# A recurrent-memory attention with a gated MLP: the output projection's last set in two column parts, K's first set inside the first Q group, the second selection in another PSUM bank

## The chip, the cores and the metric

The kernel runs on one core of a Trainium2 chip. The metric is the device time of one execution in microseconds (us); less is better. The core's engines are TensorE (PE in the profile; PEld for its weight loads), VectorE (DVE), ScalarE (ACT), GpSimd (POOL) and SyncE (SP), which issues most DMAs. They run at the same time and wait for each other by semaphores: counters that an engine raises when an instruction ends, and that another engine's instruction waits to reach a value. SBUF is the working memory. PSUM is the small memory that matmuls write; it has 8 banks here, each 512 fp32 columns wide on 128 partitions.

## The reference, cut to what matters

A sequence of 2048 tokens is cut into 64 segments of 32. Each segment is attended together with 8 memory rows, and the first 8 rows of a segment's output projection are the next segment's memory. So each segment starts only when the one before has ended. The MLP branch and the gate do not depend on that recurrence.

```python
def _A_ref(x, mem0, Wq, Wk, Wv, Wo, seg_len):
    ...
    mem = mem0
    outs = []
    for s in range(n_seg):
        xs = x[:, s * seg_len:(s + 1) * seg_len, :].copy()
        h = jnp.concatenate([mem, xs], axis=1)
        q = jnp.einsum('btd,dhe->bhte', h, Wq)
        k = jnp.einsum('btd,dhe->bhte', h, Wk)
        v = jnp.einsum('btd,dhe->bhte', h, Wv)
        scores = jnp.einsum('bhqe,bhke->bhqk', q, k) * scale
        scores = jnp.where(mask[None, None], scores, -1000000000.0)
        p = _softmax(scores, axis=-1)
        o = jnp.einsum('bhqk,bhke->bhqe', p, v)
        o = jnp.einsum('bhte,hed->btd', o, Wo)
        mem = o[:, :M, :].copy()
        outs.append(o[:, M:, :])
    return jnp.concatenate(outs, axis=1)
...
x = A_x
g = _sigmoid((x * gate_w).sum(-1, keepdims=True))
a = _A_ref(x, A_mem0, A_Wq, A_Wk, A_Wv, A_Wo, A_seg_len)
b = _B_ref(x, B_w1, B_b1, B_w2, B_b2)
return g * a + (1 - g) * b
```

There are 32 heads of 128 channels, the model width is 512, and M is 8.

## The kernel before, in words

The kernel has two stages. The first (to about 90 us) runs the MLP of some of the token tiles and loads the weights; the second is the loop over the 64 segments (line 756), which fills the rest. The order of work on every engine is the order in which the program was written: nothing is rescheduled. The framework adds the semaphore waits.

A tile T is 128 tokens, so four segments (si = 0 to 3). A segment's 32 working rows are the 8 memory rows and its first 24 tokens; the last 8 tokens of the four segments of a tile ("left" tokens) are worked on together, ahead of time, as filler work. The tile `hT` (three copies: `hc` is this segment's, `hn` the next one's) holds the 32 rows transposed, in four blocks of 128 model channels, kc = 0 to 3. Its columns 24 to 31 are the memory, written by the boundary described below.

The unit of TensorE work is a **set**: four matmuls with 32 columns of weights each, on the four column groups of the array, that run beside each other and write the four 32-partition quarters of one PSUM bank. A segment does, in this order:

1. Q and K (lines 777 to 786). Four groups, Q of heads 0 to 15 in bank U[0], K of these in U[1], Q of heads 16 to 31 in U[2], K of these in U[3]; each group is four sets, one for each kc (`qk_unit`, line 125), of 512 columns. When a group is complete ScalarE casts the bank (`qk_cast`, line 133) and VectorE transposes it into QT or KT (`qk_tr`, line 137). After the first group VectorE puts a mask into U[0] (`mask_put(1)`, line 259).
2. Scores of the first half of the heads into bank SbF (`scores(s, 0)`, line 266), exponentials, V (`v_unit`, line 147), the sums over E, the scores of the second half, and E times V (`av`, lines 290 and 295). `mask_put(0)` sets the bank SbF up for the next segment: the mask, and zeros for the columns `xs8` (sums) and `xs8z` (16 columns for the selections, next item).
3. The output projection of the memory rows (`wo_pass`, line 736): eight sets of 512 columns into bank X2 (`wo_group`, line 155). ScalarE copies the bank to the tile `w` in three pieces, columns 0 to 127, 128 to 255 and 256 to 511 (line 741).
4. The boundary to the next segment (lines 850 to 859, `new_mem`, line 744). Three **selections** transpose the 8 memory rows out of `w` into `hn`: matmuls of 8 columns (line 750) and a VectorE copy into `hT` (line 752). Selection 0 makes kc = 0 in U[0], selection 1 makes kc = 1 in U[1], selection 2 makes kc = 2 and 3 in `xs8z` of the bank SbF. Between them stand sets of filler work (`run(1)`): left tokens' Q, K or V, the left tokens' output projection, or MLP work. Then the next segment's first Q set begins.

The other engines' chains (the normalisation on GpSimd through a DMA, line 734; the loads) run beside this.

Of the kernel before, what the change touches and what calls it, by code (L numbers as in the profile page):

```python
# [10 lines left out]
BF16 = mybir.dt.bfloat16  # L11
# [17 lines left out]
def kernel(ctx, tc, A_x, A_mem0, A_Wq, A_Wk, A_Wv, A_Wo, A_seg_len, B_x, B_w1, B_b1, B_w2, B_b2, gate_w, out):  # L29
    nc = tc.nc  # L30
    P = 128
    _, S, Dm = A_x.shape
    H, Dh = A_Wq.shape[1], A_Wq.shape[2]
    M = A_mem0.shape[1]
# [4 lines left out]
    KC = Dm // P  # L39
# [5 lines left out]
    NG = H // 4  # L45
    NP = H // 2
    EW = 56
# [14 lines left out]
    Wo_sb = pers.tile([P, H, Dm], BF16)  # L62
# [11 lines left out]
    ep = early.enter_context(tc.tile_pool(name="ep", bufs=1))  # L74
# [3 lines left out]
    KL = [ep.tile([P, SPT, 2, 2, LEFT, 4, 2], BF16, name=f"KL{i}") for i in range(2)]  # L78
    VP = [ep.tile([P, SPT, 2, Dh], BF16, name=f"VP{i}") for i in range(2)]

    MkF = ep.tile([P, 4 * EW + NG + 2 * M], BF16)
    Mk = MkF[:, 0:4 * EW].rearrange("p (a c) -> p a c", c=EW)
    BO = ep.tile([P, P], BF16)
    SelM = ep.tile([P, M], BF16)
# [26 lines left out]
    U = [lps.tile([P, 512], FP32, name=f"U{i}") for i in range(4)]  # L111
    X1 = lps.tile([P, 512], FP32)
    X2 = lps.tile([P, 512], FP32)
    SbF = lps.tile([P, 512], FP32)
    W = lps.tile([P, 512], FP32)
# [9 lines left out]
    def qk_unit(bk, G, t, hf, kc):  # L125
        h0, h1 = HF[hf]
        for j in range(4):
            nc.tensor.matmul(bk[32 * j:32 * j + 32, :], lhsT=G[:, kc, :], rhs=W5[t][:, kc, h0:h1, j, :],  # L128
                             start=(kc == 0), stop=(kc == KC - 1), tile_position=(0, 32 * j))
# [22 lines left out]

    HORD = [(j, ih) for j in (0, 2, 1, 3) for ih in range(2)]

    def wo_group(bk, U_, n):
        j, ih = HORD[n]
        for c in range(4):
            i = 4 * ih + c
            nc.tensor.matmul(bk[32 * c:32 * c + 32, :], lhsT=U_[:, j, i, :], rhs=Wo_sb[:, 4 * i + j, :],  # L159
                             start=(n == 0), stop=(n == NW - 1), tile_position=(0, 32 * c))  # L160

    NW = len(HORD)

# [3 lines left out]
    def flush(q, n=1):  # L167
        for _ in range(min(n, len(q))):
            q.pop(0)()
# [39 lines left out]
    def c_load(T):  # L209
        c = cw.tile([P, Dm], BF16, tag="c", name="c")  # L210
        nc.sync.dma_start(c[:], c_dr[T * P:(T + 1) * P, :])
        cs[T] = c
# [30 lines left out]
    def prep_h(s):  # L243
        T, si = divmod(s, SPT)
        nc.gpsimd.tensor_copy(out=hT[s % 3][:, :, 0:RIDE], in_=xTs[T][:, :, seg * si:seg * si + RIDE])
# [9 lines left out]


    def mask_put(i2):
        c = 4 * EW + (NG + 2 * M if i2 == 0 else 0)
        nc.vector.tensor_copy(out=(SbF, U[0])[i2][:, 0:c], in_=MkF[:, 0:c])

    def scores(s, i2):
# [344 lines left out]
    UT = [lp.tile([P, 4, NG, 32], BF16, name=f"UT{i}") for i in range(2)]  # L606
# [25 lines left out]
    def side(T, si):  # L632
        gens = []
        if si == 2:
            gens = [wo_left(T - 1, X1) if T >= 1 else mlp_units(8)]
        elif T + 1 == NT:
            gens = [mlp_units(4)] if si < 2 else []
        else:
            gens = [[left_qk(T + 1, 0, 0, X1), left_qk(T + 1, 1, 0, U[3])], [left_qk(T + 1, 0, 1, X1), left_qk(T + 1, 1, 1, U[3])], [],
                    [left_v(T + 1, 0, X1), left_v(T + 1, 1, U[3])]][si]  # L640
        return chain(*gens)
# [53 lines left out]
    XRs, Rbs = {}, {}  # L695

    xs8 = SbF[:, 4 * EW:4 * EW + NG]
    xs8z = SbF[:, 4 * EW + NG:4 * EW + NG + 2 * M]
    RW = 9 * NG

    def xsums(E, h):
# [31 lines left out]
            for h in range(2):  # L733
                nc.gpsimd.tensor_tensor(out=out[:, :, 4 * h:4 * h + 4, o:o + b - a], in0=XR[:, :, 4 * h:4 * h + 4, a:b], in1=Rb[:, h, :, :, a:b], op=ALU.mult)  # L734

    def wo_pass(U_, cuts=(0, Dm), bk=W):
        for n in range(NW):
            wo_group(bk, U_, n)
        w = cw.tile([P, Dm], BF16, tag="w", bufs=8, name="w")
        for a, b in zip(cuts, cuts[1:]):  # L740
            nc.scalar.copy(out=w[:, a:b], in_=bk[:, a:b])  # L741
        return w

    def new_mem(w, hn, n):

        k0, nk = ((0, 1), (1, 1), (2, 2))[n]
        bk = (U[0][:, 0:M], U[1][:, 0:M], xs8z)[n]
        for k in range(nk):
            for c in range(4):
                nc.tensor.matmul(bk[32 * c:32 * c + 32, M * k:M * k + M], lhsT=w[:, (k0 + k) * P + 32 * c:(k0 + k) * P + 32 * c + 32], rhs=SelM[:],  # L750
                                 start=n < 2, stop=True, skip_group_check=True, tile_position=(0, 32 * c))
        nc.vector.tensor_copy(out=hn[:, k0:k0 + nk, RIDE:32], in_=bk.rearrange("p (k m) -> p k m", k=nk))  # L752


    WS = ((2, 2, 1), (2, 2, 2), (2, 2, 2), (2, 2, 2))
    for s in range(nseg):
        T, si = divmod(s, SPT)
        last = s == nseg - 1
        hc, hn = hT[s % 3], hT[(s + 1) % 3]
        W1, W2, W3 = WS[si]  # L760
        fill = side(T, si)
        if s + 1 < nseg:
            prep_h(s + 1)
        if s >= 1:
            x_norm(s - 1)
        if si == 0 and T >= 2:
            c_load(T - 2)
        if si < 3:
            vp_load(T, si + 1)
        if last:  # L770
            c_load(T - 1)
            c_load(T)
        if si == 0 and T + 2 < NT:
            load_xT(T + 2)
        if s in (2, (NT - 1) * SPT):
            hm_load4()
        for n, (t, hf) in enumerate(((0, 0), (1, 0), (0, 1), (1, 1))):
            bk = U[n]
            for kc in range(KC):
                qk_unit(bk, hc, t, hf, kc)  # L780
            if n == 0:
                flush(act_q, 9)
                flush(dve_q, 9)
            qk_tr(qk_cast(bk[:]), (QT, KT)[t], hf, LEFT * (1 - t))
            if n == 0:
                mask_put(1)
        V = cw.tile([P, NG, Dh], BF16, tag="V", name="V")
        E = cw.tile([P, NG, EW], BF16, tag="E", name="E")
        R = cw.tile([P, NG * 40], FP32, tag="R", name="R")
        Rs[s] = R  # L790
        xsum = SbF[:, 0:32 * NG].rearrange("p (i q) -> p i q", q=32)

        def exps(i2, x):
            c = slice(0, 40) if x else slice(40, EW)
            nc.scalar.activation(out=E[:, 4 * i2:4 * i2 + 4, c], in_=Sb[i2][:, :, c], func=ACTF.Exp, scale=scale)  # L795

        def msum(i2):
            sums(U[1 + 2 * i2][:, 320:352].rearrange("p (i q) -> p i q", q=8), E[:, 4 * i2:4 * i2 + 4, :], 40, 48, 8, True)

        def mnorm(i2):  # L800
            r, e = RP[i2], E[:, 4 * i2:4 * i2 + 4, 40:56].rearrange("p i (a q) -> p i a q", q=8)
            nc.vector.reciprocal(out=r, in_=U[1 + 2 * i2][:, 320:352])
            nc.vector.tensor_tensor(out=e, in0=e, in1=r.rearrange("p (i q) -> p i q", q=8).unsqueeze(2).to_broadcast([P, 4, 2, 8]), op=ALU.mult)

        scores(s, 0)
        nc.scalar.activation(out=E[:, 0:4, :], in_=Sb[0], func=ACTF.Exp, scale=scale)
        for kc in range(KC):
            v_unit(X1, hc, 0, kc)

        def v_cast(vb, h):  # L810
            i0 = 4 * vb + 2 * h
            nc.scalar.copy(out=V[:, i0:i0 + 2, :].rearrange("p i e -> p (i e)"), in_=(X1, X2)[vb][:, 256 * h:256 * h + 256])  # L812

        v_cast(0, 0)
        v_unit(X2, hc, 1, 0)
        if not last:
            xsums(E, 0)
            msum(0)
            mnorm(0)
        scores(s, 1)  # L820
        exps(1, 0)
        v_cast(0, 1)
        exps(1, 1)
        for kc in range(1, KC - 1):
            v_unit(X2, hc, 1, kc)
        if not last:
            if s:
                next(mlp, None)
            msum(1)
            mnorm(1)  # L830
        v_unit(X2, hc, 1, KC - 1)
        for h in range(2):
            v_cast(1, h)
        if last:
            break
        run(W1)
        if s:
            next(mlp, None)
        xsums(E, 1)
        recip_x(s)  # L840
        av(s, V, E)
        for j in (0, 2, 1, 3):
            nc.scalar.copy(out=UT[s % 2][:, j, :, 0:M], in_=U[j][:, 0:NG * 40].rearrange("p (i q) -> p i q", q=40)[:, :, 32:40])  # L843
        x_raw(s)
        run(W2)
        prep_q(s + 1)
        w = wo_pass(UT[s % 2], (0, P, 2 * P, Dm), X2)
        if s >= 1:
            ws[s - 1] = w
        run(W3)  # L850
        for _ in extra(T, si):
            pass
        new_mem(w, hn, 0)
        run(1)
        new_mem(w, hn, 1)
        run(1)
        new_mem(w, hn, 2)
        for _ in fill:
            pass
        if si == 3 and T + 2 < NT:  # L860
            left_x(T + 2)
        flush(dve_q, 9)
        nc.vector.tensor_tensor(out=rmin[:, 0:RW], in0=rmin[:, 0:RW], in1=R[:, 0:RW], op=ALU.min)
        flush(act_q, 9)
# [32 lines left out]
    wl, c = wls.pop(T), cs.pop(T)  # L897
# [26 lines left out]
    for _, bk, cc in parts:  # L924
        for i in range(SPT):
            nc.tensor.matmul(bk[32 * i:32 * i + 32, cc], lhsT=SelL[:, 32 * i:32 * i + 32], rhs=wl[:, cc], start=True, stop=False,
                             skip_group_check=True, tile_position=(0, 32 * i))
        for i in range(si):
            nc.tensor.matmul(bk[32 * i:32 * i + 32, cc], lhsT=SelR[:], rhs=ws[SPT * T + i][:, cc], start=False, stop=True,
                             skip_group_check=True, tile_position=(0, 32 * i))  # L930
# [127 lines left out]
```

## Time and profile before

| | |
|---|---|
| runs | 759.16, 757.16, 758.92 us; median 758.92 |
| profiled execution | 759.91 us, of which the profile's span is 758.1 us |
| TensorE busy | 741.6 us (98%), granted clock 0.999 |
| ScalarE, VectorE, GpSimd busy | 537.3 us (71%), 398.5 us (53%), 274.8 us (36%) |
| one segment in mid-run (402.00 to 412.23 us) | 10.23 us, TensorE busy 10.23 us |

How to read it. The busy time of TensorE is a union of matmul records, and one record of 512 columns is some 0.38 us long, while the next set starts after 0.22 us: records overlap, so a pause of TensorE shorter than about 0.17 us does not show as idle time. Pauses are read from the starts of sets in the timeline instead. A row of the timeline gives start (us), duration (us), engine, line, operation, output and inputs, the count of merged instructions, and in brackets the engine's idle time before it with what ended that. "DVE hT L752" as a releaser is the copy of a selection into hT.

### The profile page before, as it was taken

What the parts mean: (1) busy time and instruction counts of PE and PEld (TensorE: products, weight loads), DVE (VectorE), ACT (ScalarE), POOL (GpSimd) and SP (SyncE); (2) the same over time, 40 slices, a digit from 0 to 9 for tenths busy, and PEclk for the clock granted to TensorE, in tenths of its full rate; (3) what the DMA queues carried; (4) which work ended last, traced back from release to release, by engine and by line L of the source; (5) the groups of instructions that cost most, each with busy time, mean ns of one, the idle gap of its engine ahead of it and who ended that gap; (6) DMA issues with size and microseconds to landing.
All of it is one profiled execution on the core that took longest, in us unless ns stands there. A gap on an engine that the chain in (4) does not pass through costs nothing.

```text
span 758.1 us, 45047 instructions
## 1 busy us (share of the span) xinstructions
PE 741.6 (98%) x19742; PEld 423.4 (56%) x19742; DVE 398.5 (53%) x1414; ACT 537.3 (71%) x1628; POOL 274.8 (36%) x517
## 2 busy tenths in 40 slices
PE   8999999999999999999999999999999999999997
PEld 5776455555555555555555556555555555555554
DVE  5767544545455545446454545445454545455454
ACT  5667677777777777777777777776777777677764
POOL 4001234433344343344333443434443344333441
PEclk9999999999999999999999999999999999999999
DMA  9999523222222323222222213231222212222222
GB/s 294 333 309 334 154 74 63 68 85 77 72 66 67 91 67 94 66 82 60 82 78 75 85 36 99 67 83 57 76 77 84 82 56 74 66 87 70 62 81 61
DMA packets 74971, 75.70 MB, mean 100 GB/s; under 512 B 42505, under 2 KB 64882, under 8 KB 73234
## 3 DMA queue, kind: packets, MB, share of 16 engines
q1 hardware_dynamic: 73730, 71.07, 30.7%
q8 instruction: 156, 2.56, 1.4%
q0 software_dynamic: 496, 1.18, 0.7%
q10 hardware_dynamic: 544, 0.52, 0.2%
q14 instruction: 45, 0.37, 0.2%
HBM read 59.49 MB, written 6.98 MB: 88 GB/s over the span
## 4 chain that ended last, share of the span: by engine, by line
PE 86%; issue 1%; ACT 0%; DVE 0%; DMA 0%; POOL 0%; DVEq 0%
PE U L128 33%; PE X L159 18%; PE X L147 17%; PE X L128 4%; PE U L290 3%; PE W L678 2%; PE U L147 2%; PE U L266 1%; PE U L750 1%; PE SbF L266 1%; PE SbF L705 1%; PE U L295 1%; PE U L277 1%; PE U L280 0%; PE U L270 0%
## 5 line engine op out<-in xcount | busy, mean ns | idle before, releaser
L734 POOL TENSOR_TENSOR UT<-XR,Rb 128x384 bf16<-128x384 bf16 x126 | 140.3, 1136 | 309.0 <-DMA Rb<-r_dr 237.8
L133 ACT CAST Tb<-U 128x512 bf16<-128x512 f32 x288 | 168.7, 586 | 81.8 <-PE U L128 78.9
L128 PEld LDWEIGHTS <-hT 128*32 128x32 bf16 x4096 | 107.6, 96 | 100.5 <-DVE hT L752 8.1
L147 PE MATMUL X<-Wv_sb,hT 128*32 128x512 bf16 x2048 | 144.6, 378 | 0.3 <-issue 0.2
L128 PE MATMUL U<-Wq_sb,hT 128*32 128x512 bf16 x2048 | 136.5, 381 | 0.2 <-DVE hT L752 0.2
L128 PE MATMUL U<-Wk_sb,hT 128*32 128x512 bf16 x2048 | 133.1, 379 | 0.0
L159 PE MATMUL X<-Wo_sb,UT 128*32 128x512 bf16 x2016 | 121.1, 380 | 0.0
L752 DVE CAST hT<-U 128x8 bf16<-128x8 f32 x126 | 20.9, 166 | 166.1 <-PE U L750 126.0
L812 ACT CAST V<-X 128x256 bf16<-128x256 f32 x256 | 88.7, 372 | 15.9 <-PE X L147 3.3
L137 DVE STREAM_TRANSPOSE QT<-Tb 128x256 f32<-128x256 f32 x128 | 56.6, 442 | 73.3 <-ACT Tb L133 72.5
L159 PEld LDWEIGHTS <-UT 128*32 128x32 bf16 x2048 | 56.4, 96 | 54.8 <-issue 14.3
L711 ACT CAST XR<-U 128x256 bf16<-128x256 f32 x252 | 78.5, 436 | 0.0
L741 ACT CAST w<-X 128x128 bf16<-128x128 f32 x189 | 44.8, 310 | 44.9 <-PE X L159 44.9
L137 DVE STREAM_TRANSPOSE KT<-Tb 128x256 f32<-128x256 f32 x128 | 57.0, 445 | 30.9 <-ACT Tb L133 23.2
L734 POOL TENSOR_TENSOR UL<-XR,Rb 128x128 bf16<-128x128 bf16 x126 | 60.3, 502 | 0.0
L147 PEld LDWEIGHTS <-hT 128*32 128x32 bf16 x2048 | 47.2, 94 | 21.6 <-issue 1.2
L726 POOL TENSOR_TENSOR racc<-racc,R 128x72 f32<-128x72 f32 x63 | 21.2, 336 | 93.6 <-DVE R L724 66.7
L843 ACT CAST UT<-U 128x64 bf16<-128x64 f32 x252 | 35.8, 226 | 26.4 <-PE U L295 26.2
L795 ACT ACTIVATE E<-U 128x64 bf16<-128x64 f32 (+1 forms) x128 | 35.0, 273 | 11.7 <-PE U L270 11.2
L480 PEld LDWEIGHTS <-w_sb 128*128 128x128 bf16 (+1 forms) x352 | 33.5, 100 | 15.1 <-issue 2.4
L750 PEld LDWEIGHTS <-w 128*32 128x32 bf16 x1008 | 23.6, 93 | 32.0 <-ACT w L741 25.2
L159 PE MATMUL X<-Wo_sb,UL 128*32 128x512 bf16 x512 | 39.4, 379 | 0.3 <-issue 0.3
(179 smaller groups left out, 1237.5 us busy)
## 6 DMA issues: line engine op xcount, KB each, us to landing
Rb<-r_dr SPq DMA_DIRECT2D x63, 512.0 KB, 4.0
Wv_sb<-in_A_Wv_dram SPq DMA_DIRECT2D x4, 1024.0 KB, 7.1
Wq_sb<-in_A_Wq_dram SPq DMA_DIRECT2D x4, 1024.0 KB, 8.7
Wk_sb<-in_A_Wk_dram SPq DMA_DIRECT2D x4, 1024.0 KB, 8.8
Wo_sb<-in_A_Wo_dram SPq DMA_DIRECT2D x4, 1024.0 KB, 11.3
VP<-VL SPq DMA_DIRECT2D x64, 64.0 KB, 3.5
hm<-h_dr SPq DMA_DIRECT2D x69, 32.0 KB, 2.1
c<-c_dr SPq DMA_DIRECT2D x16, 128.0 KB, 3.2
```

The lines of the kernel that those rows point to most:

```text
L128: nc.tensor.matmul(bk[32 * j:32 * j + 32, :], lhsT=G[:, kc, :], rhs=W5[t][:, kc, h0:h1, j, :], start=(kc == 0), stop=(kc == KC - 1), tile_ ...
L133: nc.scalar.copy(out=Tb[:], in_=bk.rearrange("p (a b e) -> p a e b", a=8, b=2))
L137: nc.vector.transpose(out=dst[:, 8 * hf:8 * hf + 8, c0:c0 + 32, :].rearrange("p a r b -> p a (r b)").bitcast(FP32), in_=Tb[:].rearrange("p ...
L147: nc.tensor.matmul(bk[32 * j:32 * j + 32, :], lhsT=G[:, kc, :], rhs=Wv5[:, kc, 4 * vb:4 * vb + 4, j, :], start=(kc == 0), stop=(kc == KC - ...
L159: nc.tensor.matmul(bk[32 * c:32 * c + 32, :], lhsT=U_[:, j, i, :], rhs=Wo_sb[:, 4 * i + j, :], start=(n == 0), stop=(n == NW - 1), tile_po ...
L480: nc.tensor.matmul(hp[:rows, 0:TB * P], lhsT=w1_sb[:, kc, fc * P:fc * P + rows], rhs=yTs[blk][:, kc, :], start=(kc == 0), stop=(kc == KC - 1))
L711: nc.scalar.copy(out=XR[:, j], in_=U[j][:, 0:NG * 40].rearrange("p (i q) -> p i q", q=40)[:, :, 0:32])
L734: nc.gpsimd.tensor_tensor(out=out[:, :, 4 * h:4 * h + 4, o:o + b - a], in0=XR[:, :, 4 * h:4 * h + 4, a:b], in1=Rb[:, h, :, :, a:b], op=ALU ...
L741: nc.scalar.copy(out=w[:, a:b], in_=bk[:, a:b])
L795: nc.scalar.activation(out=E[:, 4 * i2:4 * i2 + 4, c], in_=Sb[i2][:, :, c], func=ACTF.Exp, scale=scale)
L812: nc.scalar.copy(out=V[:, i0:i0 + 2, :].rearrange("p i e -> p (i e)"), in_=(X1, X2)[vb][:, 256 * h:256 * h + 256])
L843: nc.scalar.copy(out=UT[s % 2][:, j, :, 0:M], in_=U[j][:, 0:NG * 40].rearrange("p (i q) -> p i q", q=40)[:, :, 32:40])
```

## The change

Three edits, all at the boundary.

- The last of the eight output-projection sets is issued as two: columns 0 to 127 (four matmuls), then 128 to 511 (four matmuls). This holds for si = 1, 2, 3, not for si = 0 (`ends`, in `wo_pass` and `wo_group`).
- Selection 1 no longer goes into U[1] but into 8 further columns of `xs8z` in the bank SbF, where selection 2 is; it accumulates onto the zeros that `mask_put(0)` puts there, which is 8 columns wider.
- The first set of the K group (kc = 0, in U[1]) is issued right after the first Q set: Q0, K0, Q1, Q2, Q3, K1, K2, K3 instead of Q0 to Q3, K0 to K3.

```diff
-    MkF = ep.tile([P, 4 * EW + NG + 2 * M], BF16)
+    MkF = ep.tile([P, 4 * EW + NG + 3 * M], BF16)
...
-    def wo_group(bk, U_, n):
+    def wo_group(bk, U_, n, cuts=(0, Dm), stop=False):
         j, ih = HORD[n]
-        for c in range(4):
-            i = 4 * ih + c
-            nc.tensor.matmul(bk[32 * c:32 * c + 32, :], lhsT=U_[:, j, i, :], rhs=Wo_sb[:, 4 * i + j, :],
-                             start=(n == 0), stop=(n == NW - 1), tile_position=(0, 32 * c))
+        for a, b in zip(cuts, cuts[1:]):
+            for c in range(4):
+                i = 4 * ih + c
+                nc.tensor.matmul(bk[32 * c:32 * c + 32, a:b], lhsT=U_[:, j, i, :], rhs=Wo_sb[:, 4 * i + j, a:b],
+                                 start=(n == 0), stop=stop or n == NW - 1, skip_group_check=len(cuts) > 2, tile_position=(0, 32 * c))
...
     def mask_put(i2):
-        c = 4 * EW + (NG + 2 * M if i2 == 0 else 0)
+        c = 4 * EW + (NG + 3 * M if i2 == 0 else 0)
...
-    xs8z = SbF[:, 4 * EW + NG:4 * EW + NG + 2 * M]
+    xs8z = SbF[:, 4 * EW + NG:4 * EW + NG + 3 * M]
...
-    def wo_pass(U_, cuts=(0, Dm), bk=W):
-        for n in range(NW):
-            wo_group(bk, U_, n)
+    def wo_pass(U_, cuts=(0, Dm), bk=W, ends=(0, Dm)):
+        for n in range(NW - 1):
+            wo_group(bk, U_, n, stop=(len(ends) > 2 and n == NW - 2))
+        wo_group(bk, U_, NW - 1, ends)
...
-        bk = (U[0][:, 0:M], U[1][:, 0:M], xs8z)[n]
+        bk = (U[0][:, 0:M], xs8z[:, 2 * M:3 * M], xs8z[:, 0:2 * M])[n]
         for k in range(nk):
             for c in range(4):
                 nc.tensor.matmul(bk[32 * c:32 * c + 32, M * k:M * k + M], lhsT=w[:, (k0 + k) * P + 32 * c:(k0 + k) * P + 32 * c + 32], rhs=SelM[:],
-                                 start=n < 2, stop=True, skip_group_check=True, tile_position=(0, 32 * c))
+                                 start=n == 0, stop=True, skip_group_check=True, tile_position=(0, 32 * c))
...
+    QK4 = ((0, 0), (1, 0), (0, 1), (1, 1))
...
-        for n, (t, hf) in enumerate(((0, 0), (1, 0), (0, 1), (1, 1))):
+        for n, (t, hf) in enumerate(QK4):
             bk = U[n]
-            for kc in range(KC):
+            for kc in range(n == 1, KC):
                 qk_unit(bk, hc, t, hf, kc)
+                if n == kc == 0:
+                    qk_unit(U[1], hc, *QK4[1], 0)
...
-        w = wo_pass(UT[s % 2], (0, P, 2 * P, Dm), X2)
+        w = wo_pass(UT[s % 2], (0, P, 2 * P, Dm), X2, (0, P, Dm) if si else (0, Dm))
```

In the built program the change adds 188 matmuls and as many weight loads to TensorE (47 segments, four more of each), and nothing to the other engines.

## The prediction

> **What bounds the kernel now.** First the page: busy shares, then the chain of work that ended last.
>
> ```profile
> span 758.1 us, 45047 instructions
> ...
> PE 741.6 (98%) x19742; PEld 423.4 (56%) x19742; DVE 398.5 (53%) x1414; ACT 537.3 (71%) x1628; POOL 274.8 (36%) x517
> ...
> PEclk9999999999999999999999999999999999999999
> ...
> PE 86%; issue 1%; ACT 0%; DVE 0%; DMA 0%; POOL 0%; DVEq 0%
> ```
>
> TensorE is busy in 98% of the span at an undiminished clock, and the chain runs through it. So each time that TensorE's stream of sets is held up counts in full, unless a later pause shrinks by as much. How often the boundary runs, and what it holds up, is in the view of the selections' copy into hT by line:
>
> ```profile
> L752 DVE CAST hT<-U x126: 165/167/168, 91.2 to 740.6; 128x8 bf16<-128x8 f32 x126
> L752 DVE CAST hT<-SbF x63: 173/174/176, 91.7 to 740.8; 128x16 bf16<-128x16 f32 x63
> ...
>   PEld L128: 8.1, 47
> ```
>
> There are 63 boundaries, with copies of 0.17 us. The timeline of one, after a segment with si = 2, all engines:
>
> ```profile
> 402.01 0.61 PE L159 MATMUL X<-Wo_sb,UL 128*32 128x512 bf16 x8
> ...
> 402.24 0.71 ACT L741 CAST w<-X 128x128 bf16<-128x128 f32 x3 [0.74 <-PE X L159]
> 402.56 0.10 PEld L750 LDWEIGHTS <-w 128*32 128x32 bf16 x4 [0.43 <-ACT w L741]
> 402.56 0.19 PE L750 MATMUL U<-SelM,w 128*32 128x8 bf16 x4
> ...
> 402.60 0.39 PE L159 MATMUL X<-Wo_sb,UL 128*32 128x512 bf16 x4
> ...
> 402.81 0.18 PE L750 MATMUL U<-SelM,w 128*32 128x8 bf16 x4
> ...
> 402.84 0.39 PE L159 MATMUL X<-Wo_sb,UL 128*32 128x512 bf16 x4
> 402.87 0.44 DVE L752 CAST hT<-U 128x8 bf16<-128x8 f32 x2 [2.55 <-PE U L750]
> 403.00 0.16 PEld L750 LDWEIGHTS <-w 128*32 128x32 bf16 x8
> 403.05 0.20 PE L750 MATMUL SbF<-SelM,w 128*32 128x8 bf16 x8
> ...
> 403.10 1.11 PE L128 MATMUL U<-Wq_sb,hT 128*32 128x512 bf16 x16
> ...
> 403.36 1.01 PEld L128 LDWEIGHTS <-hT 128*32 128x32 bf16 x24 [0.17 <-DVE hT L752]
> 403.37 0.17 DVE L752 CAST hT<-SbF 128x16 bf16<-128x16 f32 x1
> ```
>
> Read the starts. Then the four Q groups and K groups of the same segment, as the timeline of TensorE alone merges them:
>
> ```profile
> 404.04 1.04 PE L128 MATMUL U<-Wk_sb,hT 128*32 128x512 bf16 x16
> 404.90 1.04 PE L128 MATMUL U<-Wq_sb,hT 128*32 128x512 bf16 x16
> ...
> 406.63 0.27 PE L266 MATMUL SbF<-QT,KT 128*32 128x40 bf16 x16
> ```
>
> Four undisturbed sets take 404.90 - 404.04 = 0.86 us, so a set takes 0.215. Two sets started at 402.01 end their turn at 402.44; selection 0 starts at 402.56, so 0.12 us is lost waiting for ScalarE's first copy of w. Between selections 0, 1 and 2 nothing is lost: a filler set (402.60, 402.84) and a selection (0.03 to 0.04) fill the 0.25 and 0.24. The first Q group takes 404.04 - 403.10 = 0.94 instead of 0.86: 0.08 is lost waiting for the copies of selections 1 and 2 into hT. So 0.20 us of a 10.23 us segment can be won here at most, 0.12 by the first edit and 0.08 by the third.
>
> After a segment with si = 0 (16 of the 63) it looks different, because another filler set follows selection 2:
>
> ```profile
> 423.60 0.19 PE L750 MATMUL U<-SelM,w 128*32 128x8 bf16 x4
> 423.63 0.40 PE L128 MATMUL U<-Wk_sb,GL 128*32 128x512 bf16 x4
> 423.84 0.21 PE L750 MATMUL SbF<-SelM,w 128*32 128x8 bf16 x8
> 423.89 0.40 PE L128 MATMUL U<-Wk_sb,GL 128*32 128x512 bf16 x4
> 424.11 1.05 PE L128 MATMUL U<-Wq_sb,hT 128*32 128x512 bf16 x16
> 424.97 1.05 PE L128 MATMUL U<-Wk_sb,hT 128*32 128x512 bf16 x16
> ...
> 423.69 0.41 DVE L752 CAST hT<-U 128x8 bf16<-128x8 f32 x2 [2.56 <-ACT w L741]
> ```
>
> The Q group takes 0.86 there: nothing to win for the K set.
>
> **The second selection in SbF, the part that decides.** Selections 1 and 2 now share the bank SbF. Before, selection 2's matmuls into SbF ran while VectorE copied selection 1 out of U[1]: 403.05 lies inside the copies' 402.87 to 403.31. In the built program of the changed kernel selection 2's first matmul waits, at all 63 boundaries, until VectorE's count includes the copy of selection 1; before, it waited only for `mask_put(0)`, over by then (VectorE had been idle for 2.55 us). The columns are disjoint, the bank is not, and the wait goes by the bank. What queues behind: selection 2's other matmuls and all of the next segment on TensorE. VectorE and ScalarE only get their work later.
>
> How long: the copy of selection 1 ends at 402.87 + 0.44 = 403.31. It can't come sooner, since selection 1 keeps its place and the copy follows that of selection 0 on VectorE. From the copy's end to TensorE going on takes 0.05: the same copy releases the second Q set's weights at 403.36. So selection 2 starts at 403.36 instead of 403.05. It takes 403.10 - 403.05 = 0.05, so Q0 starts at 403.41. Now the sets run through: K0 403.63, Q1 403.84, Q2 404.06. Q2 needs selection 2's copy, which ended 0.49 after selection 2's start (403.37 + 0.17 - 403.05), so at 403.85, plus 0.05: in time. The fifth set starts at 403.41 + 0.86 = 404.27 instead of 404.04. **Each such boundary costs 0.23 us**: 0.31 of a new wait, less the 0.08 that it swallows. For si = 0: copies' end 423.69 + 0.41 = 424.10, plus 0.05, less 423.84: **0.31**, with no pause to swallow. Bounds for the 0.05: 0 (the wait sits on a matmul whose weights are already loaded, a form of which the trace has no case that counts) and 0.10 (twice the row); I keep the row's value. Over 63 boundaries the bounds are 3.2 us to either side.
>
> The Trainium skill, "PSUM — Partial Sum Buffer", section "Summary: rules for kernel authors", advises for reading PSUM while a matmul runs to target a different bank and to guard by bank; that is against this edit. No run here shows yet that the guard costs anything; by the rule the sum is the one above, and with waits by columns it would be the second rival's.
>
> Selection 1 itself now waits for `mask_put(0)`, which is over; `mask_put(0)` copies 256 columns instead of 248:
>
> ```profile
> L259 DVE CAST SbF<-MkF 128x248 f32<-128x248 bf16 x64 | 26.9, 421 | 2.2
> ```
>
> That is at most 421 x 8 / 248 = 14 ns, before VectorE's 2.55 us of idle time, so nothing; without that cover 0.9 us in all.
>
> **The last set in two parts.** It adds 188 matmuls and weight loads, and as many columns as before stream. In the built program ScalarE's first copy of w still waits for the count that the last matmul of the 384-column part raises; the 128-column part raises none. So the first copy starts no sooner, and the 0.12 us stays. The cost of the extra issue: a set of 8 columns has its successor 0.04 us behind it (402.56 to 402.60), and 128 columns at 0.215 / 512 a column take 0.054, more than that. So the floor is nothing; the top is a whole 0.04 for each of 47, 1.9 us. I take 0.2 in all, near the floor, because sets of 256 columns come at half the pace of 512 where they stand in a row:
>
> ```profile
> 408.55 0.28 PE L678 MATMUL W<-w_sb,hm 128*32 128x256 bf16 x4
> 408.66 0.20 PE L277 MATMUL U<-E,BO 128*32 128x32 bf16 x4
> ```
>
> (0.11 from one start to the next.) The Trainium skill, "Perfetto Trace Analysis", section "Matmuls", holds larger matmuls to be more efficient than smaller ones, where possible; by that the top end would be nearer.
>
> **K's first set inside the first Q group.** No instruction is added. In its new place it covers the wait for selection 2's copy: without it Q2 would be wanted at 403.84 and wait until 403.90. That 0.06 is in the numbers above. U[1] is free by then: its last readers stood ahead of the w copies on ScalarE. The price is that the first Q group ends one set, 0.215, later against the rest, so Q's cast and transpose, `mask_put(1)` behind them on VectorE, and K's transpose behind that:
>
> ```profile
> 404.26 0.58 ACT L133 CAST Tb<-U 128x512 bf16<-128x512 f32 x1 [0.41 <-PE U L128]
> 404.88 0.45 DVE L137 STREAM_TRANSPOSE QT<-Tb 128x256 f32<-128x256 f32 x1 [1.20 <-ACT Tb L133]
> 405.25 0.37 DVE L259 CAST U<-MkF 128x224 f32<-128x224 bf16 x1
> 405.75 0.45 DVE L137 STREAM_TRANSPOSE KT<-Tb 128x256 f32<-128x256 f32 x1
> ```
>
> K's transpose ends at 406.20, 0.43 before the scores at 406.63. With Q's part 0.215 later the mask ends at 405.62 + 0.215 = 405.84, against K's transpose wanted at 405.75: some 0.1 later, and 0.3 of cover is left. Hence nothing; without the cover it would be as many times 63 us as it is late.
>
> **Sum**: 47 x 0.23 + 16 x 0.31 + 0.2 = 10.8 + 5.0 + 0.2 = 16.0 us. The profiled execution took 759.91 (span 758.1, the rest around it), so it would become 775.9; the median of the runs shown is 1.0 lower, so I forecast 758.92 + 16.0 = **774.9**.
>
> **Rivals.**
> - *As forecast, and more*: the later Q chain runs out of its cover and the scores wait. For: ScalarE has fillers' casts to do there too. Against: 0.3 us of cover remains. If the chain is 0.1 late beyond its cover, 63 x 0.1 = 6.3 us more: 781.
> - *The other side, faster*: the wait on the bank is over when TensorE gets to it, and ScalarE's copy starts after the 128-column part. The price is then a gain of 47 x (0.12 + 0.08) = 9.4 us: 749.5. It decides only if selection 1's copy ends before 403.00, 0.31 sooner than now. Against: the program's waits, and a copy that can't start before selection 1's matmuls end at 402.99.
> - *The change does little*: the new wait is there, but pauses elsewhere in the segment shrink by as much. For: 0.12 us is lost at 402.44. Against: that wait starts from TensorE's own last set and moves along with it. If half were given back: 767.
>
> **How the numbers follow.** Forecast 0.82, more 0.07, faster 0.05, little 0.06. The forecast's own range is 774.9 less 3.2, plus 3.2 and 1.9: 771.7 to 780. I widen it to 769 and 781, part of the way to the neighbours. About 0.3% (2.3 us) is what a measurement of this kernel can tell from no change. Slower 0.93 (forecast, more, nearly all of "little"), same 0.02 (the rest of "little"), faster 0.05.
>
> **What would show it.** Right: in the timeline of a boundary, selection 2 starts some 0.3 us later after its filler set than before, with VectorE's copy of selection 1 named as what TensorE waited for; the first Q set to the last runs at 0.215 a set; the first copy of w starts as late after the projection's last set as before; segments near 10.47 us. Wrong: selection 2 directly behind its filler set, selection 0 directly behind its two fillers, or a new wait ahead of the scores.

## The result, and the profile after

| | before | changed |
|---|---|---|
| median of 6 runs each | 760.10 us (757.16 to 763.25) | 770.02 us (769.14 to 771.67) |
| ratio of the two, 95% interval | | 1.0132 (1.0103 to 1.0160) |
| profiled execution, its span | 759.91, 758.1 us | 771.67, 769.8 us |

The change makes the kernel slower, by 9.9 us between the medians and 11.8 us between the two profiled executions. The forecast was 16.0 us slower.

The page of the changed kernel, busy shares, clock and instruction queue:

```profile
span 769.8 us, 45349 instructions
...
PE 748.3 (97%) x19920; PEld 436.4 (57%) x19930; DVE 397.7 (52%) x1414; ACT 537.2 (70%) x1628; POOL 275.1 (36%) x517
...
PEclk9999999999999999999999999999999999999999
...
q8 instruction: 157, 2.57, 1.4%
```

The clock is as before and the other engines are as busy as before. The timeline of a boundary after a segment with si = 2 (columns as in the prediction: start, us, engine, line, operation):

```profile
408.68 0.62 PE L160 MATMUL X<-Wo_sb,UL 128*32 128x512 bf16 x8
408.91 0.71 ACT L743 CAST w<-X 128x128 bf16<-128x128 f32 x3 [0.65 <-PE X L160]
409.23 0.10 PEld L752 LDWEIGHTS <-w 128*32 128x32 bf16 x4 [0.43 <-ACT w L743]
409.23 0.19 PE L752 MATMUL U<-SelM,w 128*32 128x8 bf16 x4
...
409.49 0.18 PE L752 MATMUL SbF<-SelM,w 128*32 128x8 bf16 x4
...
409.51 0.39 PE L160 MATMUL X<-Wo_sb,UL 128*32 128x512 bf16 x4
409.54 0.17 DVE L754 CAST hT<-U 128x8 bf16<-128x8 f32 x1 [2.44 <-PE U L752]
409.68 0.09 PEld L752 LDWEIGHTS <-w 128*32 128x32 bf16 x1
409.74 0.17 DVE L754 CAST hT<-SbF 128x8 bf16<-128x8 f32 x1
...
409.96 0.21 PE L752 MATMUL SbF<-SelM,w 128*32 128x8 bf16 x8
409.96 0.12 PEld L752 LDWEIGHTS <-w 128*32 128x32 bf16 x7 [0.20 <-issue]
...
410.01 0.40 PE L128 MATMUL U<-Wq_sb,hT 128*32 128x512 bf16 x4
410.23 0.40 PE L128 MATMUL U<-Wk_sb,hT 128*32 128x512 bf16 x4
...
410.44 0.83 PE L128 MATMUL U<-Wq_sb,hT 128*32 128x512 bf16 x12
411.09 0.83 PE L128 MATMUL U<-Wk_sb,hT 128*32 128x512 bf16 x12
```

Selection 1 starts at 409.49 and its filler set at 409.51. One weight load of selection 2 starts at 409.68 (`x1`); then nothing starts on TensorE until 409.96, which is 0.05 us after VectorE's copy of selection 1 has ended (409.74 + 0.17). That interval is the same, 0.052 to 0.054 us, at all 63 boundaries, and so it is in e1 below. Before, selection 2 followed selection 1 after 0.24 us; now after 0.47. From 410.01 the Q and K sets run at 0.215 us each: the first Q group's 0.08 us of pauses is gone. Selection 0 still starts 0.55 us after the row with the two fillers starts (408.68 to 409.23), as at 402.01 to 402.56 before.

The view of waits shows this new wait under an unexpected name:

```profile
PEld L752 <- ACT w L743: 24.9, 65, 0.6
PEld L160 <- issue: 21.1, 60, 0.9
...
PEld L752 <- issue: 13.2, 61, 0.3
...
PE SbF L752 <- DVE hT L754: 0.5, 2, 0.3
```

Before, there was no row for "PEld L750 <- issue". The wait sits on a matmul between two weight loads, and the profile puts the pause down to no one ("issue"); only the last row, two cases, names VectorE's copy. The starts of the copy and of the matmul show whose it is.

For the experiments the time is split in two. A **boundary** runs from the start of the last filler set ahead of selection 0 to the start of the fifth Q or K set of the next segment, a **body** from there to the next boundary; both are worked out from the starts in the timelines, over all 63 boundaries and the 62 bodies between them.

| kernel (one profiled execution each) | boundary, median, si = 1 to 3 | si = 0 | all boundaries | all bodies | instruction packets |
|---|---|---|---|---|---|
| before | 1.82 us | 1.83 us | 116.5 us | 534.6 us | 156 |
| changed | 1.98 | 2.07 | 127.6 | 532.0 | 157 |

The boundaries got 11.1 us longer: 0.16 us after 47 segments and 0.24 us after 16. The bodies got 2.6 us shorter. The rest of the 11.7 us between the two spans, some 3.2 us, lies outside the segment loop, nearly all of it behind the last boundary. That tail takes 16.5 to 20.0 us over the kernels below, with no visible connection to what they change, so a difference of 3 us between two single spans says little.

### The profile page after: what moved, and what is told of

Same layout as the page of the kernel before. It is cut to its first block, busy times and chain, and to the rows that moved or that the text cites. A ratio compares the mean times of both kernels' runs of the same rounds, so it can differ in the third digit from the quotient of the medians.

```text
span 769.8 us, 45349 instructions
## 1 busy us (share of the span) xinstructions
PE 748.3 (97%) x19920; PEld 436.4 (57%) x19930; DVE 397.7 (52%) x1414; ACT 537.2 (70%) x1628; POOL 275.1 (36%) x517
## 5 line engine op out<-in xcount | busy, mean ns | idle before, releaser
L128 PEld LDWEIGHTS <-hT 128*32 128x32 bf16 x4096 | 115.9, 96 | 89.8
L128 PE MATMUL U<-Wk_sb,hT 128*32 128x512 bf16 x2048 | 145.9, 379 | 0.0
L128 PE MATMUL U<-Wq_sb,hT 128*32 128x512 bf16 x2048 | 145.8, 378 | 0.0
L147 PE MATMUL X<-Wv_sb,hT 128*32 128x512 bf16 x2048 | 144.6, 378 | 0.2 <-issue 0.2
L160 PEld LDWEIGHTS <-UT 128*32 128x32 bf16 x2236 | 61.1, 96 | 64.5 <-issue 20.7
L754 DVE CAST hT<-U 128x8 bf16<-128x8 f32 x63 | 10.5, 167 | 158.7 <-PE U L752 123.8
L147 PEld LDWEIGHTS <-hT 128*32 128x32 bf16 x2048 | 48.8, 95 | 19.5 <-issue 0.5
L752 PEld LDWEIGHTS <-w 128*32 128x32 bf16 x1008 | 26.1, 93 | 44.6 <-ACT w L743 24.9
L800 ACT ACTIVATE E<-U 128x64 bf16<-128x64 f32 (+1 forms) x128 | 35.0, 273 | 10.9 <-PE U L271 10.8
L128 PE MATMUL U<-Wk_sb,GL 128*32 128x512 bf16 x496 | 41.6, 377 | 0.0
```

What stands on the lines that cost most here:

```text
L160: nc.tensor.matmul(bk[32 * c:32 * c + 32, a:b], lhsT=U_[:, j, i, :], rhs=Wo_sb[:, 4 * i + j, a:b], start=(n == 0), stop=stop or n == NW - ...
```

## The experiments

Ratios are to the kernel before, run on the same chip in the same rounds; in brackets the 95% interval. Each diff is against the kernel before, unless said otherwise.

**The second edit alone** (e1): selection 1 in SbF, with the wider mask of the change.

```diff
-        bk = (U[0][:, 0:M], U[1][:, 0:M], xs8z)[n]
+        bk = (U[0][:, 0:M], xs8z[:, 2 * M:3 * M], xs8z[:, 0:2 * M])[n]
...
-                                 start=n < 2, stop=True, skip_group_check=True, tile_position=(0, 32 * c))
+                                 start=n == 0, stop=True, skip_group_check=True, tile_position=(0, 32 * c))
```

> The kernel before with the second edit alone: selection 1 in 8 columns of SbF, no column parts, K in its old place. Theory (the whole loss is TensorE's wait for VectorE's copy of selection 1): selection 2 starts 0.48 us after selection 1 as in the changed kernel (0.24 before), and without K's first set as cover some 0.02 us per boundary are lost again before the third Q set; about 12 us slower than before (47 x 0.17 + 16 x 0.24). Rival (the split set or the moved K set carry a good part of the loss): clearly less than 11 us slower.

Measured: 1.0119 (1.0096 to 1.0142), 769.97 against 761.24 us. Selection 2 starts 0.475 us after selection 1; all boundaries 128.8 us, 12.3 more than before; all bodies 532.2. The bank alone makes the loss at the boundaries, and the moved K set is worth 1.2 us of cover in the changed kernel (128.8 against 127.6). The boundaries came out as expected. The time did not: 8.7 us, with 10.8 at the upper end, is less than 12.3, and by the time alone it would be the rival. The next runs speak against that rival's cause: neither of the other two edits costs anything that can be told from none (e2, e4). Part of the difference shows in the bodies.

**The first edit alone** (e2): the last projection set in two column parts, with the functions of the change.

```diff
...
-        w = wo_pass(UT[s % 2], (0, P, 2 * P, Dm), X2)
+        w = wo_pass(UT[s % 2], (0, P, 2 * P, Dm), X2, (0, P, Dm) if si else (0, Dm))
```

> The kernel before with the first edit alone: the projection's last set in two column parts. Theory (ScalarE's first copy of w waits for the last matmul of the bank, whatever columns it reads): selection 0 still starts 0.335 us after the last filler set, and the time is the same as before, 0 to 1.9 us slower for 188 more matmuls. Rival (the copy is released by the 128-column part): selection 0 after 0.22 us, about 5 us faster.

Measured: 1.0011 (0.9988 to 1.0035). Selection 0 starts 0.336 us after the last filler set, as before (0.335). The split releases nothing; what it costs, 1.2 us between the medians, can't be told from none here.

**The changed kernel with selection 1 in a third bank** (e3), the mask as wide as before; the diff is against the changed kernel:

```diff
-        bk = (U[0][:, 0:M], xs8z[:, 2 * M:3 * M], xs8z[:, 0:2 * M])[n]
+        bk = (U[0][:, 0:M], U[2 if si else 1][:, 0:M], xs8z)[n]
...
```

> The changed kernel with selection 1 in a bank that neither selection 2 nor K's first set uses: U[2] after segments with si = 1, 2, 3, U[1] after si = 0. Theory: selection 2 follows selection 1 after 0.24 us as before, the first Q group to the fifth set takes 0.86 instead of 0.94 us at 47 boundaries; 47 x 0.07 = 3 us faster than before, some 14 us faster than the changed kernel. Rival (the moved K set, not the bank, holds the boundary up): no faster than before.

Measured: 1.0003 (0.9984 to 1.0021). Selection 2 follows after 0.241 us again, Q's first five sets take 0.861 instead of 0.937, all boundaries are 113.4 us, 3.1 less than before. So the loss is undone by the bank alone, and the K set does hide what it should. Yet the kernel is no faster than before, which was the rival's sign, though not for the rival's reason: its bodies took 537.6 us, 3.0 more. That left the question what the bodies wait for.

**The third edit alone** (e4): K's first set moved, selection 1 in U[1].

```diff
...
-            for kc in range(KC):
+            for kc in range(n == 1, KC):
                 qk_unit(bk, hc, t, hf, kc)
+                if n == kc == 0:
+                    qk_unit(U[1], hc, *QK4[1], 0)
```

> The kernel before with the third edit alone: K's first set right after the first Q set, while selection 1 stays in U[1], the bank of that K set. Theory: the K set has to wait until VectorE has copied selection 1 out of U[1], 0.04 us at 47 boundaries, as Q's second set did before; the pauses ahead of the third and fourth Q set go, so 0.03 us per boundary are won: 1 to 2 us faster than before. Rival (the K set gives full cover): 3 us faster.

Measured: 0.9989 (0.9972 to 1.0005). Boundaries 114.3 us, 2.1 less; the first five sets take 0.897 us, between 0.937 and 0.861: the K set waits for the copy out of its own bank, as expected. The time can't be told from that of the kernel before.

**What the bodies wait for.** The shortest bodies for si = 2 and 3 take 8.41 to 8.42 us in every kernel so far; single ones are up to 1.4 us longer (9.8 us before). The pauses have no releaser. One in the kernel before, between two sets of small matmuls (timeline of TensorE):

```profile
430.70 0.32 PE L290 MATMUL U<-E,V 32*128 32x40 bf16 x16
431.75 0.21 PE L295 MATMUL U<-E,VP 32*128 32x64 bf16 x4 [0.73 <-issue]
```

The matmuls at 431.75 wait for nothing that they read. The trace of the DMA packets gives a candidate: TensorE's program itself comes in packets of 16 KB, 256 instructions each, in the queue that the page calls instruction. Of the 18 pauses over 0.26 us with no releaser in the profile of before, all 18 end 1.28 to 1.56 us after such a packet has landed; at times drawn at random the last packet is 2.25 us back in the median. The trace holds a sharper sign: counted along TensorE's recorded instructions (matmuls, weight loads and semaphore instructions), all 18 pauses end at number 193 of a run of 256, that is, always at the same place in a packet. Most crossings from one packet to the next cost no such pause: the loop has 145 of them. The next kernels change the number of instructions.

**All eight projection sets in two parts of 256 columns** (e7): the same columns, 2016 more matmuls and as many weight loads.

```diff
...
-        for n in range(NW):
-            wo_group(bk, U_, n)
+        for n in range(NW):
+            for a, b in zip(parts, parts[1:]):
+                wo_group(bk, U_, n, a, b)
...
-        w = wo_pass(UT[s % 2], (0, P, 2 * P, Dm), X2)
+        w = wo_pass(UT[s % 2], (0, P, 2 * P, Dm), X2, (0, 2 * P, Dm))
```

> The kernel before, with all eight projection sets of every segment in two parts of 256 columns: the same columns, 2016 more matmuls and weight loads. Theory (TensorE's pauses without a releaser are waits for its own instructions, which come in DMA packets of 16 KB): some 15 more packets in the instruction queue than 156, boundaries unchanged, 1 to 5 us slower, all of it in the segments' bodies. Rival (the pauses have nothing to do with the number of instructions, and the issue of a set is free): the same time.

Measured: 1.0291 (1.0261 to 1.0321), 783.51 against 760.98 us: far more than expected, 22.5 us. The page's queue, and the longest waits of TensorE in the view of waits (us in total, times, longest):

```profile
q8 instruction: 171, 2.80, 1.5%
```

```profile
PEld L159 <- issue: 24.4, 65, 1.0
...
PEld L128 <- issue: 11.8, 20, 1.2
```

(Before: "PEld L159 <- issue: 16.3, 49, 1.3" and "PEld L128 <- issue: 1.2, 4, 0.4".) 15 more packets, and all bodies together 554.6 us, 20.0 more. But the shortest bodies for si = 2 and 3 take 8.43 us instead of before's 8.41: issuing eight more sets costs 0.02 us where nothing interrupts, some 1.2 us over 63 segments. The rest comes in irregular pauses: 52 over 0.26 us without a releaser instead of 18, all 52 ending 1.2 to 1.6 us after an instruction packet has landed, and all at the same place in a run of 256 instructions (51 at number 183, one at 184; where the count stands there differs between traces, as some records can be missing ahead of the loop). Nine of them fall into boundaries, which took some 5.8 us more in all, so that "boundaries unchanged" did not hold. That decides between the two: not the sets themselves, but their instructions cost, about 1.5 us for each further packet (22.5 / 15). It is a price at the margin; the 145 crossings of the kernel before lose only some 8 us in such pauses (the intervals from start to start, less 0.1 us each), since most cost nothing. Why such a pause ends 1.2 to 1.6 us after a landing, and not at it, no run here shows.

**The first 128 columns in a bank of their own** (e5): all eight sets of columns 0 to 127 into U[0] ahead of the last 384-column set, for si = 1, 2, 3.

```diff
...
-        for n in range(NW):
-            wo_group(bk, U_, n)
+            for n in range(NW - 1):
+                wo_group(bk, U_, n, P, Dm)
+            for n in range(NW):
+                wo_group(own, U_, n, 0, P)
+            wo_group(bk, U_, NW - 1, P, Dm)
...
-            nc.scalar.copy(out=w[:, a:b], in_=bk[:, a:b])
+            src = own if own is not None and b <= P else bk
+            nc.scalar.copy(out=w[:, a:b], in_=src[:, a:b])
```

> The kernel before, with the output projection's columns 0 to 127 of all eight sets in a bank of their own (U[0], issued ahead of the last 384-column set) for si = 1, 2, 3. Theory (the first copy of w waits for the last matmul into the bank that it reads): now the copy is released some 0.16 us sooner, selection 0 starts 0.22 instead of 0.335 us after the last filler set, 47 x 0.11 = 5 us off the boundaries. Rival (ScalarE is not free sooner, or something else holds selection 0): 0.335 as before. If pauses elsewhere give part of a shorter boundary back, and with 1316 more matmuls to fetch, the time falls by less, 2 to 5 us.

A boundary of e5 in the timeline:

```profile
412.87 0.35 PE L159 MATMUL X<-Wo_sb,UT 128*32 128x384 bf16 x4
...
413.04 0.62 PE L159 MATMUL X<-Wo_sb,UL 128*32 128x512 bf16 x8
...
413.11 0.27 ACT L749 CAST w<-U 128x128 bf16<-128x128 f32 x1 [0.51 <-PE U L159]
...
413.47 0.19 PE L758 MATMUL U<-SelM,w 128*32 128x8 bf16 x4
```

Measured: 1.0219 (1.0180 to 1.0258). The first part is as expected: the copy starts before the 384-column set's matmuls end, and selection 0 starts 0.43 us after the first filler (413.04 to 413.47), the time of two sets, with no pause; the median from the last filler to selection 0 is 0.216 us. So ScalarE's copy waits for the bank and not for the columns, and 0.12 us per boundary could be had. But 167 packets come instead of 156, and all bodies take 550.3 us, 15.7 more: 1.4 us a packet. Eight of the long pauses fall into boundaries too, and all boundaries together take 115.7 us, hardly less than before's 116.5. I had written that the time would fall; the instructions cost three times what the boundary gains.

**Both of these with the K set** (e6): e5 with K's first set moved and selection 1 in U[2] (U[1] after si = 0).

> The same, with K's first set inside the first Q group and selection 1 in U[2] (U[1] after si = 0). Theory: the two gains add up at the boundaries, 47 x (0.11 + 0.07) = 8.5 us; the time falls by less, 4 to 8 us, if pauses in the segments' bodies give part of it back. Rival: the time doesn't fall below that of the kernel before.

Measured: 1.0208 (1.0178 to 1.0239). The median boundary for si = 1 to 3 is 1.66 us instead of 1.82, bodies 554.1 us, 167 packets: the rival.

**Selections 1 and 2 with their banks exchanged** (e8), to see why the copy of selection 1 came sooner in the changed kernel.

```diff
-        bk = (U[0][:, 0:M], U[1][:, 0:M], xs8z)[n]
+        bk = (U[0][:, 0:M], xs8z[:, 0:M], U[1][:, 0:2 * M])[n]
...
-                                 start=n < 2, stop=True, skip_group_check=True, tile_position=(0, 32 * c))
+                                 start=n != 1, stop=True, skip_group_check=True, tile_position=(0, 32 * c))
```

> The kernel before with the banks of selections 1 and 2 exchanged: selection 1 in SbF, selection 2 in U[1]; no bank is shared, K's first set stays in its old place. Theory (the copy of selection 1 starts 0.07 us sooner in the changed kernel because its wait for TensorE stands in the copy itself, where the kernel before has a semaphore instruction ahead of a copy that also waits for ScalarE): the copy starts 0.26 us after selection 1 instead of 0.33, selection 2 follows selection 1 after 0.24. Rival (the copy is sooner only because TensorE stands still behind it): 0.33.

The boundary in the timeline of e8:

```profile
405.63 0.18 PE L750 MATMUL SbF<-SelM,w 128*32 128x8 bf16 x4
...
405.69 0.17 DVE L752 CAST hT<-U 128x8 bf16<-128x8 f32 x1 [2.63 <-PE U L750]
...
405.87 0.20 PE L750 MATMUL U<-SelM,w 128*32 128x8 bf16 x8
...
405.89 0.17 DVE L752 CAST hT<-SbF 128x8 bf16<-128x8 f32 x1
```

Measured: 1.0019 (0.9992 to 1.0046). Selection 2 follows after 0.24 us, so TensorE doesn't stand still, and the copy of selection 1 starts 0.26 us after it (405.63 to 405.89) as in the changed kernel, not 0.33. The bank decides, and with it the form of the wait: out of U[1], which ScalarE has read, the copy waits for two engines, for TensorE in a semaphore instruction ahead of it and for ScalarE in its own; out of SbF it waits for TensorE in its own instruction, and the semaphore instruction ahead of it waits only for VectorE's own earlier work, which is over by then. Here selection 2, now in U[1], has the two-engine form, and the first five Q and K sets take 1.005 us instead of 0.937: the 0.07 has moved.

**The changed kernel once more** (after_again).

> The changed kernel once more, for more runs beside those of the kernel before. Theory (11 us more at the boundaries, 2 to 3 us fewer pauses for TensorE's instructions in the segments' bodies): 8 to 10 us slower. Rival (the bodies don't give anything back, the first comparison was chance): 11 us or more.

Measured: 1.0143 (1.0114 to 1.0172), 768.36 against 758.27 us; boundaries 127.6 us, bodies 531.4.

**A version without the split set** (e9): K's first set moved, selection 1 in U[2] (U[1] after si = 0); e3 with the projection as before (the diff is against e3).

```diff
-        w = wo_pass(UT[s % 2], (0, P, 2 * P, Dm), X2, (0, P, Dm) if si else (0, Dm))
+        w = wo_pass(UT[s % 2], (0, P, 2 * P, Dm), X2)
```

> The kernel before with K's first set inside the first Q group and selection 1 in a third bank (U[2], after si = 0 in U[1]), without the split set. Theory: 3 us less at the boundaries, of which the bodies' pauses give a part back: 0 to 3 us faster than before. Rival (the split set's 376 instructions hid a bigger gain): more than 3 us faster.

A boundary in its timeline:

```profile
404.23 0.19 PE L752 MATMUL U<-SelM,w 128*32 128x8 bf16 x4
...
404.48 0.18 PE L752 MATMUL U<-SelM,w 128*32 128x8 bf16 x4
...
404.72 0.20 PE L752 MATMUL SbF<-SelM,w 128*32 128x8 bf16 x8
404.77 0.39 PE L128 MATMUL U<-Wq_sb,hT 128*32 128x512 bf16 x4
404.99 0.39 PE L128 MATMUL U<-Wk_sb,hT 128*32 128x512 bf16 x4
```

Measured: 0.9973 (0.9954 to 0.9992), 756.32 against 758.27 us: faster than both kernels, by 2 us against the one before, as expected. It differs from e3 only by the split set; the two intervals overlap, so what that set costs stays open. Selections at 0.25 and 0.24 us, no pause behind them, boundaries 112.7 us, 3.7 less.

**Each selection as one matmul with 128 columns of weights** (e10), the same result with 1512 instructions fewer.

```diff
-            for c in range(4):
-                nc.tensor.matmul(bk[32 * c:32 * c + 32, M * k:M * k + M], lhsT=w[:, (k0 + k) * P + 32 * c:(k0 + k) * P + 32 * c + 32], rhs=SelM[:],
-                                 start=n < 2, stop=True, skip_group_check=True, tile_position=(0, 32 * c))
+            nc.tensor.matmul(bk[:, M * k:M * k + M], lhsT=w[:, (k0 + k) * P:(k0 + k) * P + P], rhs=SelM[:],
+                             start=n < 2, stop=True, skip_group_check=True)
```

> The kernel before with each selection as one matmul with 128 columns of weights instead of four with 32: the same result, 756 matmuls and 756 weight loads fewer, six packets of 16 KB of TensorE's instructions. Theory (each packet of instructions costs TensorE about 1.5 us of pauses, as 15 more packets cost 22.5 us): five or six packets fewer, 5 to 9 us faster, by shorter bodies. Rival (the pauses come from the split sets themselves, not from the count of instructions): the same time, or slower by the switch between four narrow weight loads and a wide one.

A boundary in its timeline:

```profile
415.64 0.40 PE L159 MATMUL X<-Wo_sb,UL 128*32 128x512 bf16 x4
415.97 0.18 PE L749 MATMUL U<-SelM,w 128*128 128x8 bf16 x1
416.08 0.40 PE L159 MATMUL X<-Wo_sb,UL 128*32 128x512 bf16 x4
416.41 0.21 PE L749 MATMUL SbF<-SelM,w 128*128 128x8 bf16 x2
416.55 0.40 PE L128 MATMUL U<-Wq_sb,hT 128*32 128x512 bf16 x4
```

Measured: 1.0311 (1.0279 to 1.0344). A filler set holds the next selection back by 0.33 us (415.64 to 415.97) instead of 0.215, and the selection holds the next set back by 0.11 instead of 0.03. The Trainium skill, "TensorEngine Tiling (Array Packing)", section "Key Properties", says that changing the tiling mode drains TensorE; these 0.1 us at each change agree. All boundaries take 144.6 us, 28.1 more. The bodies take 526.0 us, 8.6 less, with 150 packets, and 4 long pauses at packet crossings are left of 18; but longer boundaries also give the packets more time, so how much of it the six packets are isn't settled.

**The last two together** (e11).

> The last two together: selections in one matmul each, K's first set inside the first Q group, selection 1 in a third bank. Theory: 5 to 11 us faster than before. Rival: no faster than the better of the two alone.

Measured: 1.0310 (1.0278 to 1.0342), boundaries 144.6 us: the rival, the drain covers all that the K set could.

## Why the prediction was right in direction and mechanism, and where it was off

- **The new wait on the bank**: right in place and cause. e1 and e3 show it from both sides: with the bank alone it is there, with the bank alone undone it is gone. The Trainium skill's rule that the prediction cited ("PSUM — Partial Sum Buffer", section "Summary: rules for kernel authors"), to guard by bank, is what the built program does; the guard costs 0.235 us here (0.476 from selection 1 to 2 instead of 0.241). These waits are semaphores that the framework put in; what the chip would do without them no run shows.
- **Its size is the term that was off.** I took 0.31 us per boundary because the copy of selection 1 "can't come sooner", as it follows the copy of selection 0. It does come sooner. The row `402.87 0.44 ... x2` holds two copies of 0.167 us, so 0.10 us between them is VectorE waiting (the second runs from 403.14 to 403.30), and I read it as work back to back. In the kernel before, the copy of selection 1 ends 0.49 us after selection 1's start; in the changed kernel 0.42 after (409.49 to 409.91; medians 0.492 and 0.423). The reason is that with the move to SbF its wait for TensorE stands in the copy itself and no longer in a semaphore instruction ahead of it (e8). Now it does run back to back: it starts 0.03 us after the copy of selection 0 has ended (409.54 + 0.17 to 409.74). The 0.05 from the copy's end to TensorE is right (409.91 to 409.96). With 0.07 less at 63 boundaries the sum of 15.8 becomes 11.4; measured at the boundaries are 11.1. So the time that was measured lies outside what the terms themselves allowed (771.7 to 780): my bounds were on the 0.05, which was right, and none stood on the copy. That 770.02 lies inside the wider range, from 769, is luck as far as the mechanism goes.
- **What the bodies gave back** was not in the sum. In the three kernels with the new wait as in the change (changed, once more, e1) all bodies together took 531.4 to 532.2 us; in before, e2, e3, e4, e8 and e9, at 156 or 157 packets, 533.6 to 537.6. That is 1.4 us or more. The long pauses at packet crossings lose 6.0, 5.1 and 6.5 us in the bodies of these three, 8.4 in those of the kernel before and 6.5 to 8.2 in the others, so much of what was given back is these pauses. That packets land in time while TensorE stands at the boundary would explain it, but it is argued, not shown. It can account for the step from 11.1 to the 9.9 and 10.1 between the medians, which the tail's scatter can do as well: the intervals of the two comparisons alone would allow 11.1; e1's doesn't allow its 12.3.
- **The split set**: right that it releases nothing, for the reason given (the copy waits for the bank's last matmul; e2, e5). Its price of 0.2 us was worked out from set times alone; 376 instructions are one and a half packets, 2 us by e7's price, and e2's interval (up to 0.35%) holds both.
- **K's first set**: right in kind. It hides 3.1 us where no wait stands in front of it (e3), near the 0.08 us for each of 47 that the prediction read, and 1.2 us beside the new wait (e1 against the changed kernel), about half of the 0.06 for each that it put there. That it would not make the scores wait is right too: no such pause follows, and the shortest bodies take 8.42 us, as before within 0.01.
- **The rivals**: "as forecast, and more" did not come; "the other side" failed on the bank, as its condition said; "the change does little" was wrong in size but had a true core: a pause elsewhere does shrink. I had looked for it at selection 0, and it was in the bodies.
- **What would show it**: I expected VectorE's copy to be named for the pause; the profile calls it "issue" in nearly all cases.

## What to carry to other kernels

Where the program's waits go by PSUM bank, as here, two transfers through one bank are one queue: before putting a second one there, look at who reads the first and when that ends, and take a bank that nobody is reading, even if its columns must be found elsewhere. Where TensorE is the bound, count its instructions as well as its columns: here each further packet of 256 cost about 1.4 us, so an edit that splits many sets must win more than that. And before you put two merged rows down as work back to back, compare the row's length with that of its single instructions. Also read short pauses of TensorE from the starts of sets, since neither the busy share nor the view of waits names them.

## What the runs showed of the hardware that was not expected

- TensorE waits for its own instructions. 15 more packets of 16 KB brought 20.0 us more in the bodies (e7) and 11 more 15.7 (e5), though the sets themselves cost 0.02 us a segment; the long pauses without a releaser end 1.2 to 1.6 us after such a packet has landed and at one and the same place in a run of 256 instructions (all 18 in the loop of the kernel before, all 52 in e7).
- A VectorE copy that has its wait for TensorE in a semaphore instruction ahead of it, since the copy itself waits for ScalarE, starts later than one that waits for TensorE in its own instruction: for selection 1, 0.33 us after the matmuls began (before) and 0.26 (e8, where the copy ahead of it limits it too); for selection 2, with VectorE idle before the copy, 0.385 (e8) and 0.27 (changed).
- Between sets of four 32-column weights and a matmul with 128 columns, TensorE loses 0.1 us at each change (e10).
- With the wait, and nearly the same number of instructions, the times scatter less: 769.1 to 771.7 us over six runs of the changed kernel, 757.2 to 763.3 over six of the one before.
